# Moving three score tiles and one transpose block in the TensorE order of a fused attention and mixture-of-experts kernel

## The chip, the cores and the metric

The kernel runs on one core of one Trainium2 chip. The metric is device time in microseconds (us) of one execution. The core has five engines that run their own instruction streams in order and wait for each other through semaphores: TensorE (PE in the rows; its weight loads are PEld), VectorE (DVE), ScalarE (ACT), GpSimd (POOL) and SyncE (SP), which issues loads.

## The reference, cut to what matters

Attention with normalised queries and keys feeds a mixture-of-experts layer; q, k and v are 8 x 12 x 448 x 64 in float32 (batch, heads, tokens, head size).

```
q_n, k_n = rmsnorm(q, g_q), rmsnorm(k, g_k)
scores   = (q_n @ k_n.T) / sqrt(64)
x        = softmax(scores) @ v              # 3584 tokens x 768
y_dense  = relu(x @ w1_dense) @ w2_dense    # 768 -> 512 -> 768
expert   = argmax(x @ w_gate)               # 8 experts
y_moe    = gate * (relu(x @ w1[expert]) @ w2[expert])
out      = y_dense + y_moe                  # 3584 x 768, float32
```

## The kernel before, in words

**Units of work.** The 12 heads of a batch are three groups of four heads, so there are 24 groups, g = 0 to 23. A group has seven score tiles, s0 to s6. `scores` (L336 to L350) makes one: TensorE writes a tile of 128 x 2 x 448 into one of two PSUM buffers called `sc`, and ScalarE takes its exponential into `xflat`, which frees the buffer. A tile takes two matmuls, each over 64 of the 128 rows of the array; s3 takes four, each over a quarter of the array. `attend` (L366) multiplies the exponentials with the values into the PSUM tile `AV`, `division` divides, `xtrans` (L407) turns the result, x, with eight transposes into bank 1 of the PSUM tile `W`, and `xturned` copies it to `xT`. `logits` (L425) are eight small matmuls for the gate.

**Preparing a group.** GpSimd adds the squares up (`ss`, L290, from the square `m` that ScalarE makes at L288), ScalarE makes the scale r from it with a logarithm and an exponential (`ln`, L294, and `r`, L296), GpSimd multiplies with r (`xn`, L302, four instructions a group), and TensorE turns the product with 28 transposes (L313) into both banks of `W`. They are followed on TensorE by value products and the next score tiles. On GpSimd's queue stand, between the `xn` of one group and the `ss` of the next, a scatter of finished records (L488) and two casts of v (L267).

**Dense chunks.** When a batch's x is there, its 448 tokens go through `w1_dense` in four chunks of 128, 128, 128 and 64 tokens (`dense`, L616): six matmuls of 512 columns a chunk, accumulated in one bank of `W`; `relu` (L624) on ScalarE takes the sum out and frees the bank. The first and third chunk use bank 0, the second and fourth bank 1. The chunks of a batch are spread over the score tiles of the following batches' groups. Below, **place A** is the second chunk, **place B** the third. Both occur in the six batches from the first to the sixth while scores still run.

**What sets the order.** All instructions of the attention part are issued in the order of a list of times (`AT`, L16 on). A group is 7 units of that time long; an entry is an offset, one for each of the three kinds of group (g mod 3). `s0` to `s6` give the score tiles, `de` the chunks: for each its bank, its parts as (time, first matmul, last matmul + 1), the time of its relu and of its scatter. An instruction's place on every engine follows from that order; TensorE and ScalarE run theirs in it strictly. After 161 units the order is a written list, `tail`. The part behind it works through expert tiles on TensorE.

Of the kernel before, what the change touches and what calls it, by code (L numbers as in the profile page):

```python
# [17 lines left out]
AT = {'p00': [-0.862, 1.524, -1.092],  # L18
# [28 lines left out]
 'own': {1: -12.564, 2: 120.5, 13: 150.009, 14: 144.215, 15: 158.423, 16: None, 17: None, 18: None},  # L47
 'bl': 11.7,
 'last': 25,
# [39 lines left out]
def kernel(  # L89
# [94 lines left out]
    tail = const.tile([P, NT, 2], I32)  # L184
# [91 lines left out]
    def stats(g, name, s0, s1):  # L276
        if g >= NG:
            return []
        if g not in sts:
            sts[g] = sb.tile([P, 2, J, 2, 3], F32, tag="st", name="st")  # L280
        return [lambda s=s: nc.vector.bn_stats(  # L281
            sts[g][:, "qk".index(name), s].rearrange("p h c -> p (h c)"),
            xin[name, g].rearrange("p h (s d) -> p s d h", d=D)[:, s]) for s in range(s0, s1)]
# [14 lines left out]
    def normalise(g, name, hh, eng=None, r=None):  # L298
        r = rs[g] if r is None else r
        if (name, g) not in xn:  # L300
            xn[name, g] = sb.tile([P, J, 2, D], BF16, tag="xn" + name, name="xn", bufs=1)
        (eng or nc.gpsimd).tensor_tensor(  # L302
            xn[name, g][:, :, hh], xin[name, g][:, hh].rearrange("p (s d) -> p s d", d=D),
            r[:, "qk".index(name), :, hh].unsqueeze(2).to_broadcast([P, J, D]), ALU.mult)
# [78 lines left out]
    def division(g, r):  # L383
        b, gb = divmod(g, NB)
        if gb == 0 and r == 0:
            xas[b] = rb[b % 3][:, :, :XH].bitcast(BF16)
            xTs[b] = xT2[b % 2]
        claim("av", ("av", g, r))
        inv = sb.tile([P, 2, 4, 1], F32, tag="inv", name="inv")
        x = xas[b][:, :, gb * 256:gb * 256 + 256].rearrange("p m (a h i) -> p h m a i", a=2, h=4)  # L390

        def head(hh):
            on("AV", nc.vector.tensor_tensor(  # L393
                x[:, 2 * hh + r], av[:, hh, :, :D].rearrange("p m (a i) -> p m a i", a=2),
                inv[:, hh].unsqueeze(3).to_broadcast([P, 4, 2, 32]), ALU.mult), hh)
            if hh == 1:
                free(("av", g, r))

        return [lambda: on("AV", nc.vector.reciprocal(inv, av[:, :, :, D:]), 0, 1), lambda: head(0),
                lambda: head(1)]  # L400
# [74 lines left out]
    def places(b):  # L475
        rk = W[:, 1, RK:].rearrange("p (m e) -> p m e", e=E)
        at = ats[b % 2]

        def summed():
            with nc.allow_low_precision(reason="whole numbers"):  # L480
                nc.vector.tensor_reduce(slot[b % 2], at, AX.X, ALU.add)

        return [lambda: (on("W", nc.vector.tensor_tensor(at[:, :, :E], rk, oh[:, b, :4], ALU.mult),
                            1), free(("ra", b))),
                summed]
# [179 lines left out]
    def put(t, key, n, make):  # L665

        got = []

        def run(i):
            if not got:  # L670
                got.extend(make())
                assert len(got) == n, (key, n, len(got))
            got[i]()

        t0, dt = t if isinstance(t, tuple) else (t, 0.001)
        for i in range(n):
            todo.append((t0 + i * dt, len(todo), key, lambda i=i: run(i)))

    def put1(t, key, f, *a):
        put(t, key, 1, lambda: [lambda: f(*a)])  # L680
# [7 lines left out]
    def shift(t, z):  # L688
        return (t[0] + z, t[1]) if isinstance(t, tuple) else t + z

    def at(name, z, g):
        t = AT[name]
        return shift(t[g % NB] if isinstance(t, list) else t, z)

    def attention():
        for g in range(NG):
            z = J * g
            if g:
                for s in range(J):
                    put1(at("s%d" % s, z - J, g), ("s", g, s), scores, g, s)  # L700
            for r in range(2):
                for i, (m0, m1) in enumerate(((0, 2), (2, 4))):
                    put1(at("p%d%d" % (r, i), z, g), ("p", g, r), attend, g, r, m0, m1)
                put(at("d%d" % r, z, g), ("d", g, r), 3, lambda g=g, r=r: division(g, r))
            put1(at("xt", z, g), ("xt", g), xtrans, g)
            put1(at("xe", z, g), ("xe", g), xturned, g)
            put1(at("lo", z, g), ("lo", g), logits, g)
            if g > 1:
                put1(at("tr", z - 14, g), ("tr", g), transposes, g)
                put1(at("tq", z - 14, g), ("tq", g), turned_q, g)  # L710
                put1(at("tk", z - 14, g), ("tk", g), turned_k, g)
                put1(at("va", z - 7, g), ("va", g), values, g)
            if g > 2:
                put(at("st", z - 21, g), ("st", g), 14,
                    lambda g=g: stats(g, "k", 0, 7) + stats(g, "q", 0, 7))
                put1(at("me", z - 21, g), ("me", g), means, g)
                put1(at("no", z - 21, g), ("no", g), norms, g)
                put(at("nm", z - 21, g), ("nm", g), 4, lambda g=g: [
                    lambda name=name, hh=hh: normalise(g, name, hh)
                    for name in AT["kq"] for hh in range(2)])  # L720
                put1(at("lv", z - 14, g), ("lv", g), load_v, g)
            if g > 4:
                put1(at("lq", z - 35, g), ("lq", g), load_q, g)
                if g % 2 == 0:
                    put1(at("lk", z - 35, g), ("lk", g), load_k, g)
        for b in range(B):
            z = J * NB * (b + 1)
            put(at("ch", z, 0), ("ch", b), 8, lambda b=b: choose(b))
            put1(at("ra", z, 0), ("ra", b), ranks, b)
            put(at("pl", z, 0), ("pl", b), 2, lambda b=b: places(b))  # L730
            put(at("ga", z, 0), ("ga", b), 4, lambda b=b: gates(b))
            for m, bank, ks, re, se in AT["de"]:
                for t, k0, k1 in ks:
                    put1(z + t, ("de", b, m), dense, b, m, bank, k0, k1)
                put1(z + re, ("re", b, m), relu, b, m, bank)
                put1(AT["sx"].get((b, m), z + se), ("se", b, m), scatter, b, m)
        for n, job in enumerate(wjobs):
            if n >= 1:
                t = AT["we"][0] + (n - 3) * AT["we"][1]
                if n in AT["own"]:  # L740
                    t = AT["own"][n]
                if t is not None:
                    put1(t, ("we", n), nc.gpsimd.dma_start, *job)
        put(AT["el"], ("el",), 21, early_list)
        put1(AT["bl"], ("bl",), blank)
        todo.sort()
        for t, _, key, f in todo:
            if t < J * (NG - 1):
                f()
            else:  # L750
                left.setdefault(key, []).append(f)
# [286 lines left out]
    with tc.manual_schedule(engines=ENGINES):  # L1038
        prologue()
        attention()  # L1040
        tail_and_slots()
# [42 lines left out]
```

## Time and profile before

| what | us |
|---|---|
| median of 3 runs | 353.22 |
| lowest and highest run | 351.29, 355.0 |
| the profiled execution, its own time | 350.3 |
| its span on the core | 348.6 |
| TensorE busy in the span | 312.8 |
| ScalarE busy in the span | 212.8 |
| attention with dense chunks under way, about | 56 to 200 |
| expert tiles, about | 212 to 345 |

An engine's busy time is the time in which at least one of its instructions runs. Matmuls overlap each other, so a busy TensorE is not one at its peak. Times in the rows are counted from the start of the span.

### The profile page before, as it was taken

Reading aid. Unit: us, or ns where it says so; the run is one execution under the profiler, and the core shown is the slowest. Engines: PE = TensorE matmul, PEld = TensorE weight load, DVE = VectorE, ACT = ScalarE, POOL = GpSimd, SP = SyncE. Lnnn points to the kernel's source line nnn. Section 1 sums busy time; section 2 is a strip of 40 time slices with the busy share of each in tenths; the row PEclk is TensorE's granted clock in tenths of the full one; section 3 lists DMA queues with packets and bytes.
Section 4 is the critical chain, followed back from the end, with each engine's and each line's share of the span. In section 5 each row is a group of like instructions: output and inputs, shape, how many; then the busy total and the mean of one; then the engine's idle time right before and its main releaser. Section 6 shows DMA issues by size and latency. Waiting matters only on the chain. (4 is left out here: it accounts for less than half of the span.)

```text
span 348.6 us, 11328 instructions
## 1 busy us (share of the span) xinstructions
PE 312.8 (90%) x4164; PEld 192.7 (55%) x4164; DVE 231.4 (66%) x835; ACT 212.8 (61%) x348; POOL 202.2 (58%) x290
## 2 busy tenths in 40 slices
PE   0389989989989899999899899999999999999990
PEld 0255656656656565666666556555555555555550
DVE  5988998878988879888898744258222226364641
ACT  2389998898898898998988834322332332323220
POOL 4666887788886987988987522462323221322222
PEclk9999999999999999999999999999999999999997
DMA  7999999999997999989999799999999948495422
GB/s 263 265 249 240 311 291 210 289 259 323 233 305 240 256 300 253 285 227 253 262 276 192 166 186 182 259 282 248 176 248 240 212 121 205 123 182 140 123 93 80
DMA packets 83406, 78.85 MB, mean 226 GB/s; under 512 B 46894, under 2 KB 76088, under 8 KB 83344
## 3 DMA queue, kind: packets, MB, share of 16 engines
q1 hardware_dynamic: 69360, 42.58, 50.8%
q0 software_dynamic: 13984, 35.47, 40.5%
q8 instruction: 36, 0.59, 0.7%
q14 instruction: 26, 0.21, 0.2%
HBM read 61.40 MB, written 23.02 MB: 242 GB/s over the span
## 5 line engine op out<-in xcount | busy, mean ns | idle before, releaser
L350 ACT ACTIVATE xflat<-sc 128x896 bf16<-128x896 f32 x168 | 143.8, 918 | 6.0 <-PE sc L348 5.4
L302 POOL TENSOR_TENSOR xn<-we,r 128x448 bf16<-128x448 f32 x90 | 82.0, 945 | 14.5 <-issue 6.8
L348 PE MATMUL sc<-qT,kT 64*128 64x448 bf16 (+1 forms) x384 | 65.9, 372 | 12.0 <-ACT xflat L350 8.8
L366 PE MATMUL AV<-va,xflat 128*128 128x65 bf16 (+1 forms) x1536 | 75.7, 195 | 0.5 <-ACT xflat L350 0.4
L281 DVE BATCH_NORM_STATS2 st<-we 128x6 f32<-128x128 f32 x336 | 70.3, 280 | 2.9 <-DMA we<-in_k_dram 2.8
L366 PEld LDWEIGHTS <-xflat 128*128 128x128 bf16 (+1 forms) x1536 | 59.9, 98 | 22.2 <-issue 12.1
L929 POOL DMA_INDIRECT out_dram<-xflat,tail x22 | 22.7, 1032 | 64.5 <-DVE xflat L928 52.4
L928 DVE COPY xflat<-yp 128x768 f32<-128x768 f32 x22 | 21.0, 956 | 46.3 <-PE yp L898 46.3
L878 ACT COPY heT<-AV 128x512 bf16<-128x512 bf16 x26 | 15.2, 585 | 55.3 <-PE AV L874 55.3
L488 POOL DMA_INDIRECT records<-rall,slot x32 | 33.1, 1036 | 23.7 <-ACT rall L624 18.0
L616 PE MATMUL W<-wd,xT 128*128 128x512 bf16 (+1 forms) x240 | 42.8, 339 | 0.7 <-DVE kT L334 0.7
L898 PE MATMUL yp<-we,heT 128*128 (+1 forms) x232 | 42.5, 326 | 0.0
L348 PEld LDWEIGHTS <-kT 64*128 64x128 bf16 (+1 forms) x384 | 24.1, 97 | 28.3 <-issue 22.0
L393 DVE TENSOR_TENSOR rall<-AV,inv 128x256 bf16<-128x256 f32 x96 | 36.3, 420 | 1.7
L859 PE MATMUL W<-we,xflat 128*128 (+1 forms) x132 | 32.6, 379 | 0.3 <-issue 0.2
L624 ACT ACTIVATE rall<-W 128x512 bf16<-128x512 f32 (+1 forms) x40 | 20.3, 509 | 19.9 <-PE W L616 18.4
L887 PE MATMUL yp<-wd,xflat 128*128 128x384 bf16 x176 | 32.2, 327 | 0.0
L864 ACT ACTIVATE hs<-W,tail 128x512 bf16<-128x512 f32 x26 | 17.9, 687 | 23.1 <-PE W L859 19.5
L898 PEld LDWEIGHTS <-heT 128*128 128x128 bf16 (+1 forms) x304 | 22.5, 97 | 15.0 <-issue 1.0
L267 POOL CAST va<-we 128x448 bf16<-128x448 f32 x48 | 26.9, 593 | 0.0
L616 PEld LDWEIGHTS <-xT 128*128 128x128 bf16 (+1 forms) x240 | 16.8, 102 | 15.3 <-issue 4.4
L887 PEld LDWEIGHTS <-xflat 128*128 128x128 bf16 x176 | 16.9, 98 | 14.1 <-issue 1.3
(151 smaller groups left out, 348.6 us busy)
## 6 DMA issues: line engine op xcount, KB each, us to landing
we<-in_moe_w_dram POOLq DMA_DIRECT2D x16, 768.0 KB, 10.0
we<-in_q_dram SPq DMA_DIRECT2D x24, 448.0 KB, 9.6
we<-in_k_dram SPq DMA_DIRECT2D x11, 896.0 KB, 8.2
we<-in_v_dram SPq DMA_DIRECT2D x48, 128.0 KB, 9.6
we<-in_v_dram SPq DMA_DIRECT2D x48, 96.0 KB, 7.2
wd<-in_moe_w_dense_dram POOLq DMA_DIRECT2D x2, 768.0 KB
we<-in_k_dram SPq DMA_DIRECT2D x2, 448.0 KB, 3.5
records<-rall,slot POOLq DMA_INDIRECT x32, 6.6
```

The costliest lines, as they stand in the source:

```text
L267: nc.gpsimd.tensor_copy(vas[g % 3][:, :, :, a * 32:a * 32 + 32].rearrange("p s h i -> p h s i"), xin["v", g].rearrange("p h (s i a) -> p h ...
L281: return [lambda s=s: nc.vector.bn_stats(sts[g][:, "qk".index(name), s].rearrange("p h c -> p (h c)"), xin[name, g].rearrange("p h (s d) - ...
L302: (eng or nc.gpsimd).tensor_tensor(xn[name, g][:, :, hh], xin[name, g][:, hh].rearrange("p (s d) -> p s d", d=D), r[:, "qk".index(name), : ...
L348: nc.tensor.matmul(ps[out, hh, :S], kT[row, w:w + out.stop - out.start], qT[row, r], start=True, stop=True, skip_group_check=True)
L350: nc.scalar.activation(x, ps[:, :, :S], AF.Exp, scale=scale)
L366: on("AV", nc.tensor.matmul(av[:, hh, m], exs[g, s][rows_, hh, QC[m]:QC[m] + P], va[rows_, s, hh, :De], start=(first and s == full[0] and ...
L393: on("AV", nc.vector.tensor_tensor(x[:, 2 * hh + r], av[:, hh, :, :D].rearrange("p m (a i) -> p m a i", a=2), inv[:, hh].unsqueeze(3).to_b ...
L488: i = nc.gpsimd.indirect_dma_start(out=rec, out_offset=bass.IndirectOffsetOnAxis(ap=slot[b % 2][:, m:m + 1], axis=0), in_=rb[b % 3][:, m], ...
L616: on("W", nc.tensor.matmul(o, xTs[b][:, kk, q0:QC[m] + P], wd1[:, kk, c], start=(kk == 0), stop=(kk == KD - 1), skip_group_check=(m == 3)) ...
L859: got = [nc.tensor.matmul(he[c], xRs[t][:, kk, c], matrix(t, 0, h, kk * F, (kk + 1) * F), start=(kk == 0), stop=(kk == KD - 1)) for h, c i ...
L887: nc.tensor.matmul(yps[t][:, dd, :HD], xRs[t][:, KD + i], wd2[:, i, dd * HD:(dd + 1) * HD], start=(i == 0), stop=False, skip_group_check=True)
L898: return [nc.tensor.matmul(yp[c, dd, :HD], heTs[t][:, i, c], matrix(t, 1, h, cols.start, cols.stop), start=False, stop=(i == FT - 1), skip ...
```

## The change

Three entries of the table change, and one is new.

- At place A the tile s3 of the group that follows (offset 0.9, now 0.65) comes between the second and the third matmul of the second dense chunk. It stood behind that chunk's relu.
- At place B the third dense chunk is cut in two parts, matmuls 0 and 1 and matmuls 2 to 5, and the tile s0 of the group that follows (offset 0.455, now -0.4) comes between them. It stood behind the chunk and behind the eight logits matmuls. Of group 4, which has no chunk there, s0 moves ahead of eight logits matmuls.
- `xtrans` of group 22, the eight transposes of the last but one turn of x, stands at 160.9 in the list of times, ahead of logits and the first value products of group 23. In `tail` it stood behind them and behind two loads of expert numbers.

```diff
- 'de': ... (2, 0, [(20.56, 0, 6)], 20.943, 27.29), (3, 0, [(26.48, 0, 6)], 28.824, 32.5)],
+ 'de': ... (2, 0, [(20.56, 0, 2), (20.62, 2, 6)], 20.943, 27.29), (3, 0, [(26.48, 0, 6)], 28.824, 32.5)],
+ 'xs': {22: 160.9},
- 's0': [-0.586, 0.455, 2.566],
+ 's0': [-0.586, -0.4, 2.566],
- 's3': [0.9, 0.991, 3.16],
+ 's3': [0.65, 0.991, 3.16],
- 'tail': [..., ('nu', 0), ('nu', 1), ('xt', 22), ('de', 6, 2), ...
+ 'tail': [..., ('nu', 0), ('nu', 1), ('de', 6, 2), ...
-            put1(at("xt", z, g), ("xt", g), xtrans, g)
+            put1(AT["xs"].get(g, at("xt", z, g)), ("xt", g), xtrans, g)
```

The changed kernel has one line more above these functions, so its lines have numbers higher by one. The instructions of VectorE, GpSimd and SyncE stand as before; those of TensorE and ScalarE move.

TensorE at place A of one batch, before: the last two of the chunk's six matmuls (L616) and the four matmuls of s3 (L348) behind them.

```order
L616 LDWEIGHTS xT_82
L616 MATMUL W<-wd_88,xT_82 128x512
L616 LDWEIGHTS xT_82
L616 MATMUL W<-wd_88,xT_82 128x512
L348 LDWEIGHTS kT_92
L348 MATMUL sc<-qT,kT_92 64x448
L348 LDWEIGHTS kT_92
L348 MATMUL sc<-qT,kT_92 64x448
L348 LDWEIGHTS kT_92
L348 MATMUL sc<-qT,kT_92 64x448
L348 LDWEIGHTS kT_92
L348 MATMUL sc<-qT,kT_92 64x448
```

The same place now: the first two of the six, then s3, then the other four (one of them shown).

```order
L617 LDWEIGHTS xT_82
L617 MATMUL W<-wd_88,xT_82 128x512
L349 LDWEIGHTS kT_92
L349 MATMUL sc<-qT,kT_92 64x448
L349 LDWEIGHTS kT_92
L349 MATMUL sc<-qT,kT_92 64x448
L349 LDWEIGHTS kT_92
L349 MATMUL sc<-qT,kT_92 64x448
L349 LDWEIGHTS kT_92
L349 MATMUL sc<-qT,kT_92 64x448
L617 LDWEIGHTS xT_82
L617 MATMUL W<-wd_88,xT_82 128x512
```

So the four remaining matmuls of the chunk, and with them its relu, come behind s3.

ScalarE over places A and B of one batch, before: `xflat<-sc` are exponentials of score tiles, the two `rall<-W` rows the relus of place A and place B.

```order
L350 ACTIVATE xflat<-sc 128x896 x2
L624 ACTIVATE rall<-W 128x512
L350 ACTIVATE xflat<-sc 128x896 x2
L288 ACTIVATE m_1471<-st 128x28
L350 ACTIVATE xflat<-sc 128x896
L294 ACTIVATE ln<-ss,eps_t 128x28
L296 ACTIVATE r<-ln 128x28
L350 ACTIVATE xflat<-sc 128x896 x2
L624 ACTIVATE rall<-W 128x512
L350 ACTIVATE xflat<-sc 128x896 x3
```

The same stretch now.

```order
L351 ACTIVATE xflat<-sc 128x896 x3
L625 ACTIVATE rall<-W 128x512
L351 ACTIVATE xflat<-sc 128x896
L289 ACTIVATE m_1471<-st 128x28
L351 ACTIVATE xflat<-sc 128x896
L295 ACTIVATE ln<-ss,eps_t 128x28
L297 ACTIVATE r<-ln 128x28
L351 ACTIVATE xflat<-sc 128x896 x3
L625 ACTIVATE rall<-W 128x512
L351 ACTIVATE xflat<-sc 128x896 x2
```

Each of the two relus now has one more exponential ahead of it and one fewer behind it.

## Rows read from the trace of the kernel before

**Rows 1.** Page, part 1: busy us, share of the span, instructions.

```profile
PE 312.8 (90%) x4164; PEld 192.7 (55%) x4164; DVE 231.4 (66%) x835; ACT 212.8 (61%) x348; POOL 202.2 (58%) x290
```

**Rows 2.** Windows: attention, expert tiles; busy us by engine (instructions), clock, DMA.

```profile
56.00:200.00 144.00, 135.75 (x2403) 88.04 (x2401) 121.90 (x486) 127.04 (x208) 120.00 (x161) 1.00 0.99 256
212.00:320.00 108.00, 106.99 (x772) 61.03 (x770) 44.81 (x108) 33.77 (x55) 33.00 (x35) 1.00 0.93 204
```

**Rows 3.** ScalarE's waits, 56 to 200: us in total, times, longest.

```profile
ACT rall L624 <- PE W L616: 11.7, 18, 1.0
ACT xflat L350 <- PE sc L348: 2.5, 9, 0.9
```

**Rows 4.** TensorE's waits, 56 to 200.

```profile
PE sc L348 <- ACT xflat L350: 5.8, 11, 1.0
```

**Rows 5.** Lines by form: a dense matmul of 512 columns; busy, mean ns | idle before.

```profile
L616 PE MATMUL W<-wd,xT 128*128 128x512 bf16 x144 | 36.2, 381 | 0.0
```

**Rows 6.** Timeline of TensorE over places A and B of one batch: start, us, what.

```profile
83.07 1.47 PE L616 MATMUL W<-wd,xT 128*128 128x512 bf16 x6
84.47 0.68 PE L348 MATMUL sc<-qT,kT 64*64 64x448 bf16 x6
84.98 0.80 PE L313 MATMUL W<-ident,xn 64*128 64x64 bf16 x28
...
86.34 0.35 PE L348 MATMUL sc<-qT,kT 64*128 64x448 bf16 x1
...
89.15 1.47 PE L616 MATMUL W<-wd,xT 128*128 128x512 bf16 x6
...
90.74 0.68 PE L348 MATMUL sc<-qT,kT 64*128 64x448 bf16 x6
...
92.11 0.36 PE L348 MATMUL sc<-qT,kT 64*128 64x448 bf16 x2
92.30 0.58 PE L313 MATMUL W<-ident,xn 64*128 64x64 bf16 x28
```

**Rows 7.** Timeline of ScalarE, same batch; in brackets idle time before and its releaser.

```profile
84.58 0.60 ACT L624 ACTIVATE rall<-W 128x512 bf16<-128x512 f32 x1 [0.77 <-PE W L616]
85.07 1.72 ACT L350 ACTIVATE xflat<-sc 128x896 bf16<-128x896 f32 x2
86.66 0.25 ACT L288 ACTIVATE m<-st 128x28 f32<-128x28 f32 x1
86.79 0.93 ACT L350 ACTIVATE xflat<-sc 128x896 bf16<-128x896 f32 x1
...
87.96 0.23 ACT L296 ACTIVATE r<-ln 128x28 f32<-128x28 f32 x1
...
90.66 0.60 ACT L624 ACTIVATE rall<-W 128x512 bf16<-128x512 f32 x1 [0.86 <-PE W L616]
...
94.55 0.32 ACT L294 ACTIVATE ln<-ss,eps_t 128x28 f32<-128x28 f32 x1
```

**Rows 8.** Timeline of GpSimd, same batch.

```profile
88.31 3.64 POOL L302 TENSOR_TENSOR xn<-we,r 128x448 bf16<-128x448 f32 x4 [1.07 <-ACT r L296]
92.11 1.06 POOL L488 DMA_INDIRECT records<-rall,slot  x1 [0.16 <-issue]
...
94.26 0.26 POOL L290 TENSOR_TENSOR ss<-st,m 128x28 f32<-128x28 f32 x1
```

**Rows 9.** Timeline of TensorE: a score matmul and the fourth chunk behind it.

```profile
94.74 0.35 PE L348 MATMUL sc<-qT,kT 64*128 64x448 bf16 x1
95.02 0.85 PE L616 MATMUL W<-wd,xT 128*64 128x256 bf16 x12
```

**Rows 10.** Timeline of ScalarE, the batch before that one.

```profile
70.64 0.32 ACT L294 ACTIVATE ln<-ss,eps_t 128x28 f32<-128x28 f32 x1 [0.74 <-POOL ss L290]
```

**Rows 11.** Timeline of GpSimd, the fifth of the six batches.

```profile
161.70 3.63 POOL L302 TENSOR_TENSOR xn<-we,r 128x448 bf16<-128x448 f32 x4 [1.34 <-DMA we<-in_v_dram]
```

**Rows 12.** Timeline of TensorE: transposes of group 22 behind loads of expert numbers.

```profile
205.31 0.62 PE L407 MATMUL W<-ident,rall 128*128 128x128 bf16 x8 [0.82 <-issue]
```

4 rows, old and new, of the table AT are left out of this document.

## The prediction

> **What bounds the kernel now.** I read the page's busy shares first. TensorE is busy for 90% of the span [rows 1]; that is an average over two stages, so the windows come next. From 212 us on TensorE is busy 106.99 of 108 us [rows 2]: whatever reaches it late there ends late, and a microsecond lost or won in attention comes out at the end as one. In attention, 56 to 200 us, TensorE (135.75 of 144), ScalarE (127.04), VectorE (121.90) and GpSimd (120.00) are all nearly full, at full granted clock. So busy shares decide nothing there and the waits must be read. ScalarE waits 11.7 us for dense chunks, 18 times, and 2.5 us for score tiles [rows 3]; TensorE waits 5.8 us for ScalarE to free a score buffer, 11 times [rows 4]. Each engine waits for the other, at different points of a batch. That is what the change aims at: while six dense matmuls run, ScalarE has emptied both score buffers and stands idle, 0.77 us at place A and 0.86 us at place B of one batch [rows 7]. The question is what comes after these two places, and I followed one batch engine by engine.
>
> **Prices on TensorE.** A dense matmul takes 0.38 us [rows 5], and six of them 1.47 [rows 6], so they start (1.47 - 0.38) / 5 = 0.218 us apart. The last one at A starts at 84.54 - 0.38 = 84.16, and s3 starts at 84.47: 0.31 after it, so going from full-array matmuls to score matmuls costs 0.09 over the pace. From s3 to the next tile it is 85.15 - 0.36 - 84.47 = 0.32; from a score matmul to a dense one 95.02 - 94.74 = 0.28 [rows 9]. A tile in the middle of a chunk thus costs one such passage more, 0.09 us, and the rest of the chunk ends 0.3 us plus that later. No row shows a tile in the middle of an accumulation; the bounds are 0 (the passage hides under the weight loads) and 0.16 a passage (the next matmul starts only when the last has ended, 0.38 - 0.22). I take 0.09, the price of the same passage at the end of a chunk.
>
> The Trainium skill has a rule that speaks against the change: TensorEngine Tiling (Array Packing), section Key Properties, says that switching the tiling mode drains TensorE. Here 0.31 us stands where a full drain would need the 0.38 us of the matmul ahead, so the trace agrees that a switch costs something and not that it empties the array. By the rule at its strictest each passage would cost 0.16 us instead of 0.09.
>
> **Place A, step by step** [rows 6 to 8]. Before: the chunk runs from 83.07 to 84.54, its relu from 84.58 to 85.18. In the shadow of the relu TensorE does s3 and the next tile (84.47 to 84.98) and starts the 28 transposes of the next group. These write both banks, so from the second on they wait for the relu; they take 0.80 us here and 0.58 us at 92.30, where nothing holds them: a stall of 0.22. Then come value products and the tile s1, whose second matmul (86.34) lets ScalarE go on at 86.79; r follows at 87.96.
> Now: two dense matmuls (83.07, 83.29), s3 at 83.60, the other four at 83.92, 84.14, 84.35 and 84.57, end 84.95 instead of 84.54, the next tile at 84.88 instead of 84.79. ScalarE has s3 at about 84.01, so most of its idle 0.77 is filled. But the relu starts at 84.99 and ends at 85.59, **0.41 later**; the stall of the transposes grows from 0.22 to 0.54, and everything behind them on TensorE is 0.41 late. ScalarE, with one exponential fewer behind the relu, reaches the square m at about 86.27 instead of 86.66, 0.39 early, and then waits: s1 ends at 86.34 + 0.41 + 0.35 = 87.10, its exponential starts at 87.14 instead of 86.79. So r is 0.35 late. What was hidden under the relu (s3 on TensorE) has been moved ahead of it, and what waits for the relu pays.
>
> **Where the 0.35 goes.** GpSimd stood idle 1.07 us for r and starts `xn` 0.12 after r has ended (88.31). Behind it the queue is close to gapless: four `xn` (3.64), the scatter at 92.11, two casts, `ss` at 94.26 to 94.52, and ScalarE's `ln` starts at 94.55. In the batch before, `ln` even waited 0.74 us for `ss` [rows 10]. So 0.35 late at r is about 0.3 late at the next `ln`, and behind that ScalarE runs through to the next place A. Four of the six batches look like this one (`xn` after an idle of 1.07). In the fifth the idle is 1.34 and ends with something else, a load of v [rows 11]: it takes up 0.27 of the delay, I count 0. In the sixth the delay stays on TensorE, which is the bound from there on: 0.4.
>
> **Place B** [rows 6, 7]. s0 starts at 89.37 + 0.31 = 89.68 instead of 90.74; the chunk ends 0.4 later, and logits and s3 keep their place within 0.1. No transposes wait for this relu: the next 28 come at 92.30, when even a relu that ends 0.4 later than 91.26 is through. ScalarE fills most of its 0.86, and the third exponential could start about 0.3 earlier. But the next `ln` waits for `ss` of GpSimd, which was set by r back at A; what B gives ScalarE is given back there. I count 0, with bounds of +0.1 (the passage) and -0.3 a batch (if `ln` could follow).
>
> **The rest.** s0 of group 4 passes eight small logits once: 0, within 0.2. The eight transposes of group 22 take 0.62 us and stand behind an idle of 0.82 us in which TensorE's sequencer loads two expert numbers [rows 12]. They move ahead of value products on the same engine; the loads stay behind the same products, so the idle stays. VectorE's copy of the turned x comes earlier, but nothing on TensorE waits for it. I count 0, between -0.8 (the idle goes) and +0.5 (the transposes are no longer ahead of a chunk but in a place where they wait).
>
> **Sum.** 4 x 0.3 + 0 + 0.4 = +1.6 us. The profiled execution took 350.3 us and would take 351.9. It lies 2.9 us under the median of the three runs, 353.22; on that the forecast is **354.8 us**. A difference under 1%, 3.5 us, can't be told from none in this kernel, so this is forecast as no change that shows, on the slower side. Chance 0.5, with its own range of 353.5 to 356.2.
>
> **Rivals.**
> - *ScalarE is the bound and its idle time comes back.* For: 11.7 us of waits for dense chunks, and TensorE's 5.8 us for ScalarE, which say that later in the batch ScalarE is last. Then the 0.39 that m is early at A and the 0.3 at B count, 6 x 0.69 = 4.1, 349.1 us. Against: s1 behind the transposes on TensorE. It decides for this rival if the second of the 28 transposes at A starts no later than now after the chunk began, 85.22 - 83.07 = 2.15 us (85.22 being the relu's end and the 0.04 us that it also took from the chunk's end to the relu). Half of it, with A lost and B kept, is 351.3. Chance 0.17, a third of it over 1%.
> - *The delay is taken up on the way.* TensorE's 5.8 us of waits for ScalarE are slack for TensorE, and GpSimd may catch up in more batches than the fifth; then only the last 0.4 or so stays, 353.2 to 354.0. Chance 0.2.
> - *The passages cost a full matmul and nothing takes them up.* A then is 0.41 + 2 x 0.07 = 0.55 late, B 0.16 late on TensorE: 6 x 0.71 = 4.3, 357.5 us, slower by 1.2%. For: the weights of a score tile and of a dense matmul replace each other in mid-accumulation, which no row shows. Against: 0.31 and 0.28 [rows 6, 9]. It decides from 0.16 us a passage on. This is also what the Trainium skill's rule on the drain (named above) gives. Chance 0.13.
>
> **Range and chances.** The likeliest case alone gives 353.5 to 356.2; to hold 8 in 10 the range reaches down to half of the first rival and to a run or two of scatter (the three runs lie within 3.7 us), and up to the last: 350.6 to 357.4. Faster by over 1%: 0.09, from the first rival and scatter; slower by over 1%: 0.13, from the last rival and scatter on the forecast; within 1%: 0.78.
>
> **What would show it.** In the changed profile the relu at A starts about 1.92 us after its chunk's first matmul instead of 1.51, with ScalarE's idle before it near 0.2; the 28 transposes behind it take near 1.1 us instead of 0.80; GpSimd's idle for r grows from 1.07 towards 1.8 (its `ss` comes 0.39 earlier and r 0.35 later); ScalarE waits near 0.6 us for s1 behind the square. At B the relu's idle shrinks from 0.86 and `ln` waits longer for `ss`. A place A comes about 0.3 us later each batch than before. The prediction is wrong if GpSimd's `xn` starts earlier after the chunk than the 5.24 us of now (88.31 - 83.07), or if place A of successive batches comes closer together; then ScalarE was the bound after all.

## The result and the profile after

The kernel before has a median of 353.17 us in 22 runs, the changed one 357.97 us in 22 runs. In half of the changed kernel's runs the time is 7 us to 21 us longer than in its shortest, in some of the kernel before 6 us to 48 us, and the comparison leaves these runs out. Of the others the ratio is **1.0066, 95% interval 1.004 to 1.0091**: +2.3 us (1.4 to 3.2) on some 352. The lowest runs, 352.77 and 350.77 us, say +2.0. The forecast was 354.8 us, +1.6, on the slower side and too small to show, in a range of 350.6 to 357.4. The median of the runs that are compared, 354.34 us, lies in it; that of all 22, 357.97, lies just above it.

The execution that was profiled has a span of 372.0 us, and only its attention part is read against the kernel before. The window of the expert tiles shows why [rows 2]; the columns are as there.

```profile
212.00:320.00 108.00, 90.76 (x601) 51.47 (x608) 34.70 (x97) 28.76 (x48) 28.18 (x31) 0.92 1.11 171
```

TensorE is busy for 90.76 of 108 us there, not 106.99, at a granted clock of 0.92. In attention the waits have changed places. ScalarE's waits, 56 to 202 us, after [rows 3]:

```profile
ACT xflat L351 <- PE sc L349: 10.9, 27, 0.8
ACT ln L295 <- POOL ss L291: 1.8, 2, 1.1
ACT rall L625 <- PE W L617: 0.3, 1, 0.3
```

The 11.7 us of waits for dense chunks are gone, as intended, and 10.9 us of waits for score tiles have come, where 2.5 were. TensorE's waits in the same stretch [rows 4]:

```profile
PE sc L349 <- ACT xflat L351: 4.2, 9, 0.9
PE W L314 <- issue: 1.3, 4, 0.4
PE W L314 <- ACT rall L625: 1.1, 3, 0.4
```

L314 are the 28 transposes; the last two rows hold their waits at the six places A, up to 0.4 us each, and one of 0.2 us behind a place B. At place A the profile names the relu (L625) three times and three times nothing ("issue"). The timeline of TensorE shows the two places of one batch [rows 6]. The second matmul of each cut chunk has no record in this trace.

```profile
83.67 0.39 PE L617 MATMUL W<-wd,xT 128*128 128x512 bf16 x1
84.20 0.38 PE L349 MATMUL sc<-qT,kT 64*64 64x448 bf16 x4
84.52 1.04 PE L617 MATMUL W<-wd,xT 128*128 128x512 bf16 x4
...
85.69 0.19 PE L314 MATMUL W<-ident,xn 64*128 64x64 bf16 x1
86.24 0.56 PE L314 MATMUL W<-ident,xn 64*128 64x64 bf16 x27 [0.36 <-issue]
...
87.36 0.35 PE L349 MATMUL sc<-qT,kT 64*128 64x448 bf16 x1
...
90.39 0.38 PE L617 MATMUL W<-wd,xT 128*128 128x512 bf16 x1 [0.16 <-issue]
90.71 0.36 PE L349 MATMUL sc<-qT,kT 64*128 64x448 bf16 x2
91.00 1.04 PE L617 MATMUL W<-wd,xT 128*128 128x512 bf16 x4
```

ScalarE in the same batch [rows 7]:

```profile
84.64 0.92 ACT L351 ACTIVATE xflat<-sc 128x896 bf16<-128x896 f32 x1 [0.23 <-PE sc L349]
85.59 0.60 ACT L625 ACTIVATE rall<-W 128x512 bf16<-128x512 f32 x1
...
86.88 0.24 ACT L289 ACTIVATE m<-st 128x28 f32<-128x28 f32 x1
87.74 0.92 ACT L351 ACTIVATE xflat<-sc 128x896 bf16<-128x896 f32 x1 [0.61 <-PE sc L349]
...
88.89 0.23 ACT L297 ACTIVATE r<-ln 128x28 f32<-128x28 f32 x1
...
92.08 0.60 ACT L625 ACTIVATE rall<-W 128x512 bf16<-128x512 f32 x1
```

And GpSimd [rows 8]:

```profile
87.21 0.24 POOL L291 TENSOR_TENSOR ss<-st,m 128x28 f32<-128x28 f32 x1 [0.39 <-ACT m L289]
89.25 3.64 POOL L303 TENSOR_TENSOR xn<-we,r 128x448 bf16<-128x448 f32 x4 [1.80 <-ACT r L297]
```

Counted from the chunk's first matmul (83.07 us before, 83.67 now), the relu starts after 1.92 us instead of 1.51, the square m after 3.21 instead of 3.59, r after 5.22 instead of 4.89, and `xn` after 5.58 instead of 5.24. ScalarE waits 0.61 us for the score tile that stands behind the transposes on TensorE. (The prediction calls that tile s1; it is s4 of its group.)

From one place A to the next (start of the relu) the traces give, in us:

| kernel | 1 to 2 | 2 to 3 | 3 to 4 | 4 to 5 | 5 to 6 | 1 to 6 |
|---|---|---|---|---|---|---|
| before | 24.72 | 24.12 | 24.81 | 24.15 | 24.25 | 122.05 |
| before, once more (`e8_before_again`) | 24.74 | 24.14 | 24.84 | 24.90 | 24.24 | 122.87 |
| the change | 25.05 | 24.47 | 25.15 | 25.09 | 24.57 | 124.33 |
| the change, once more (`e1_whole`) | 25.08 | 24.46 | 25.18 | 25.07 | 24.59 | 124.38 |

The second trace of the kernel before is needed here: the 24.15 of the fourth period stands in the first trace alone (why is read under `e8_before_again`). Against the second trace the five periods lose 0.31, 0.33, 0.31, 0.19 and 0.33 us. From the batch's first relu to the first at A 3.72 us pass instead of 3.30, and from the sixth at A to the first expert matmul 28.63 instead of 28.73 (the first trace; the second takes 30.19, at a lower granted clock). That is +1.5 + 0.4 - 0.1 = **+1.8 us** up to the expert tiles.

This sum is put together from two traces, since each of them alone holds something that is not the change's. From the first relu to the first expert matmul the kernel before takes 154.08 and 156.34 us, `e4_turn_22`, which moves nothing in these batches, 154.91, the change 156.68 and 156.78. So the change alone is +2.6 against one trace, +0.3 against the other and +1.8 against `e4_turn_22`: the periods and offsets batch by batch say more than these totals.

### The profile page after: what moved, and what is told of

Its sections match the earlier page's. It is cut to its first block, busy times and chain, and to the rows that moved or that the text cites. A ratio compares the mean times of both kernels' runs of the same rounds, so it can differ in the third digit from the quotient of the medians.

```text
span 372.0 us, 11293 instructions
## 1 busy us (share of the span) xinstructions
PE 313.2 (84%) x4129; PEld 193.0 (52%) x4164; DVE 230.5 (62%) x835; ACT 216.5 (58%) x348; POOL 202.2 (54%) x290
## 4 chain that ended last, share of the span: by engine, by line
PE 39%; DMA 10%; ACT 5%; SPq 5%; DVE 3%; issue 3%; DVEq 1%; POOL 0%; POOLq 0%; ACTq 0%
DMA rall<-records 9%; PE yp L888 7%; PE yp L899 6%; PE W L617 6%; PE W L860 6%; PE AV L367 5%; ACT xflat L351 4%; PE sc L349 4%; SPq L799 3%; PE W L408 2%; ACT rall L625 1%; DMA xflat<-records 1%; PE mid L860 1%; DVE rall L833 1%; SPq L798 1%
## 5 line engine op out<-in xcount | busy, mean ns | idle before, releaser
L351 ACT ACTIVATE xflat<-sc 128x896 bf16<-128x896 f32 x168 | 145.9, 917 | 14.9 <-PE sc L349 13.6
L349 PE MATMUL sc<-qT,kT 64*128 64x448 bf16 (+1 forms) x384 | 67.3, 371 | 12.5 <-ACT xflat L351 7.5
L617 PE MATMUL W<-wd,xT 128*128 128x512 bf16 (+1 forms) x219 | 41.6, 335 | 3.0 <-issue 1.9
L860 PE MATMUL W<-we,xflat 128*128 (+1 forms) x121 | 30.5, 379 | 0.7 <-issue 0.2
L625 ACT ACTIVATE rall<-W 128x512 bf16<-128x512 f32 (+1 forms) x40 | 20.4, 509 | 9.5 <-PE W L617 7.2
L617 PEld LDWEIGHTS <-xT 128*128 128x128 bf16 (+1 forms) x240 | 15.9, 102 | 15.8 <-issue 7.7
```

The lines of the kernel that those rows point to most:

```text
L349: nc.tensor.matmul(ps[out, hh, :S], kT[row, w:w + out.stop - out.start], qT[row, r], start=True, stop=True, skip_group_check=True)
L351: nc.scalar.activation(x, ps[:, :, :S], AF.Exp, scale=scale)
L617: on("W", nc.tensor.matmul(o, xTs[b][:, kk, q0:QC[m] + P], wd1[:, kk, c], start=(kk == 0), stop=(kk == KD - 1), skip_group_check=(m == 3)) ...
L860: got = [nc.tensor.matmul(he[c], xRs[t][:, kk, c], matrix(t, 0, h, kk * F, (kk + 1) * F), start=(kk == 0), stop=(kk == KD - 1)) for h, c i ...
```

## The experiments

The theory: place A alone loses, since its relu comes 0.41 us later and the 28 transposes, s4 and r queue behind it; place B and the turn of x move nothing. The rivals: the switches between dense and score matmuls cost TensorE time at both places; or place B takes back what A loses.

**e1_whole**: the change itself, on the chip of the next three.

> The whole change once more, beside its parts on one chip. Theory (the relu of place A stands in the path: s3 has left its shadow, the transposes wait for it, and value products, the next tile, r and GpSimd's queue follow): +1.5 to +3 us, and in the profile the relu of A about 0.41 us later than before against the m = 0 relu of the same batch, the transposes behind it taking 1.1 us. Rival 1 (ScalarE's idle time comes back): not slower. Rival 3 (passages between tiling modes): the rest of a chunk behind a tile ends over 0.5 us late at A and at B.

Measured: 1.0111 (1.0017 to 1.0205), which is +3.9 us with a wide interval; lowest run 354.28 us against 350.52. Its offsets at A are those shown above: the relu starts 1.93 us after the chunk, the transposes take 1.12 us, m comes at 3.22, r at 5.23.

**e2_place_A**: place A alone.

```diff
- 's3': [0.9, 0.991, 3.16],
+ 's3': [0.65, 0.991, 3.16],
```

> Only s3 in the middle of the second chunk; place B, s0 of group 4 and the transposes of group 22 as before. Theory: all of the loss is here, +1.5 to +3 us, as much as the whole change within 0.7 us. Rival 1: a gain of up to 2.3 us (0.39 x 6). Rival 3: half of the loss, since half of the twelve places have the tile in the chunk.

Measured: 1.004 (0.9958 to 1.0122), too wide to tell by time. The trace tells: periods of 25.09, 24.48, 25.17, 25.03 and 24.61 us, 124.37 in all, the whole change's 124.38. Each period is within 0.04 us of that of `e1_whole`, so place B and the turn of group 22 add nothing to place A. TensorE at place A of the second batch, with all its records:

```profile
83.57 0.60 PE L616 MATMUL W<-wd,xT 128*128 128x512 bf16 x2
84.10 0.38 PE L348 MATMUL sc<-qT,kT 64*64 64x448 bf16 x4
84.42 1.04 PE L616 MATMUL W<-wd,xT 128*128 128x512 bf16 x4
...
85.59 0.19 PE L313 MATMUL W<-ident,xn 64*128 64x64 bf16 x1
86.14 0.56 PE L313 MATMUL W<-ident,xn 64*128 64x64 bf16 x27 [0.36 <-issue]
```

The second dense matmul starts at 83.57 + 0.60 - 0.38 = 83.79, s3 0.31 after it, the third dense matmul 0.32 after s3. So a switch inside a chunk costs what it costs at the end of one. The chunk ends at 85.46 instead of 83.57 + 1.47 = 85.04.

**e3_place_B**: place B alone.

```diff
- (2, 0, [(20.56, 0, 6)], 20.943, 27.29)
+ (2, 0, [(20.56, 0, 2), (20.62, 2, 6)], 20.943, 27.29)
- 's0': [-0.586, 0.455, 2.566],
+ 's0': [-0.586, -0.4, 2.566],
```

> Only s0 in the middle of the third chunk (and s0 of group 4 ahead of eight logits); place A and the transposes of group 22 as before. Theory: 0, within 0.7 us, because no one waits for that relu and what ScalarE gains it gives back waiting for ss. Rival 1: a gain of up to 1.8 us (0.3 x 6). Rival 3: half of the loss, about +1 to +1.5 us.

Measured: 1.0021 (0.9947 to 1.0096). The first three periods are 24.71, 24.11 and 24.81 us, those of the kernel before to 0.03. The fifth (25.21) has a wait of VectorE for a load of q in it, 1.97 us, and isn't read; the fourth (25.33) has none and is read below. ScalarE, at place B of the second batch and at the `ln` of the third:

```profile
90.33 0.92 ACT L350 ACTIVATE xflat<-sc 128x896 bf16<-128x896 f32 x1 [0.30 <-PE sc L348]
91.30 0.60 ACT L624 ACTIVATE rall<-W 128x512 bf16<-128x512 f32 x1
...
119.80 0.32 ACT L294 ACTIVATE ln<-ss,eps_t 128x28 f32<-128x28 f32 x1 [1.14 <-POOL ss L290]
```

The relu's idle 0.86 is nearly gone (0.30 ahead of the exponential before it), and `ln` waits 1.14 us for `ss` where the kernel before waits 0.84 at that `ln`. What ScalarE gained it waits for there. In the first two batches that wait is as before (0.78 for 0.74, and none): ScalarE comes to m 0.27 us early, but to the exponential behind it only 0.03 and 0.05 early, after idle times of 0.14 and 0.12 for which the profile names nothing. In all three batches `ln` starts 0.03 to 0.04 us after `ss` has ended, and as far from the chunk at A as in the kernel before (12.28, 11.47 and 12.38 us, to 0.01), so an earlier ScalarE could not have moved it.

The fourth period is 0.43 longer than in the second trace of the kernel before, in which a score tile behind place A stops as it does here (see `e8_before_again`). TensorE, behind place B of that batch:

```profile
142.88 0.22 PE L313 MATMUL W<-ident,xn 64*128 64x64 bf16 x2 [0.22 <-issue]
...
143.64 0.97 PE L366 MATMUL AV<-va,xflat 128*128 128x65 bf16 x13 [0.36 <-DVE rall L393]
```

It stops ahead of the last two of the 28 transposes, with nothing named, and waits for VectorE's division behind them. Neither trace of the kernel before has these two waits; the change and `e1_whole` have both in the same batch (0.17 and 0.21, then 0.36), though their period there is only 0.06 and 0.04 longer than with place A alone. So the zero for place B holds in three batches and not in this one, and what stops the two transposes is not shown.

**e4_turn_22**: the turn of x for group 22 alone.

```diff
+ 'xs': {22: 160.9},
- 'tail': [..., ('nu', 0), ('nu', 1), ('xt', 22), ('de', 6, 2), ...
+ 'tail': [..., ('nu', 0), ('nu', 1), ('de', 6, 2), ...
-            put1(at("xt", z, g), ("xt", g), xtrans, g)
+            put1(AT["xs"].get(g, at("xt", z, g)), ("xt", g), xtrans, g)
```

> Only the eight transposes of group 22 ahead of logits and value products; places A and B as before. Theory: 0, within 0.5 us, the 0.8 us of idle time for the two loads of expert numbers stay, now right ahead of the dense chunk. Rival: the idle time is gone, -0.8 us.

Measured: 1.0015 (0.9961 to 1.0068); its periods are those of the second trace of the kernel before to 0.06, 122.85 us in all, the 24.96 of the fourth among them. TensorE before the expert tiles [rows 12]:

```profile
203.85 0.62 PE L408 MATMUL W<-ident,rall 128*128 128x128 bf16 x8
204.31 0.34 PE L426 MATMUL AV<-wgb,xT 128*128 128x8 bf16 x8
204.51 0.77 PE L367 MATMUL AV<-va,xflat 128*128 128x65 bf16 x16
206.13 3.54 PE L617 MATMUL W<-wd,xT 128*128 128x512 bf16 x24 [0.86 <-issue]
```

The turn stands ahead of the value products without a wait, and the idle time of 0.82 us has stayed where the number loads are: 0.86, now ahead of the chunk.

**e5_A_late_transposes**: place A, and the 28 transposes moved one stage of value products back, behind s4, so that the relu is through when they start.

```diff
- 'tr': [2.755, 1.399, 2.327],
- 'tq': [3.163, 3.396, 3.158],
+ 'tr': [2.755, 3.92, 2.327],
+ 'tq': [3.163, 3.93, 3.158],
- 's3': [0.9, 0.991, 3.16],
+ 's3': [0.65, 0.991, 3.16],
```

> Place A as in the change, and the 28 transposes that waited for its relu moved behind the next value products and the tile after them (with the copy of q behind them on VectorE). Theory: the wait for the relu is covered, so the 0.36 us a batch of e2 go and ScalarE's early exponentials count: place A to place A of the next batch no longer than before, the whole between -1.0 and +0.5 us. Rival 3 (the passages themselves are the loss): still as slow as e2, about +1.5 us or more, because the same passages are there. Rival 1 expects nothing different from e2.

Measured: 1.0024 (0.9982 to 1.0066); 122.73 us from the first to the sixth place A. With place A alone it was 124.37, before 122.05 and 122.87. TensorE, the second batch:

```profile
84.71 0.69 PE L366 MATMUL AV<-va,xflat 128*128 128x65 bf16 x13
...
85.41 0.68 PE L313 MATMUL W<-ident,xn 64*128 64x64 bf16 x28
...
87.53 0.61 PE L407 MATMUL W<-ident,rall 128*128 128x128 bf16 x8 [0.54 <-DVE kT L334]
```

The relu is as late as in place A alone (1.93 us after the chunk's start), but the transposes take 0.68 instead of 1.12 and r starts 4.50 us after the chunk, not 5.23. Value products now stand where the transposes waited. So the loss of place A is the transposes' wait and what queues behind it. By time the result is +0.8 us (-0.6 to +2.3), above the expected -1.0 to +0.5 but not clear of it. A new wait has come: TensorE stands idle 0.54 us for VectorE's copy of kT, which frees the bank for the turn of x.

**e6_late_transposes**: the late transposes without place A (the first four lines of the diff above).

> Only the 28 transposes moved behind the value products and the next tile, the tiles at A and B as before. Theory: no gain, since they waited just 0.2 us for the relu; instead the copies of q and k on VectorE come about 0.7 us later and x's transposes, which need the bank, wait for them: 0 to +2 us, so that a gain of e5 against e2 is not the move's own. Rival (the move is a gain by itself): -0.2 x 6 = -1.2 us.

Measured: 1.0064 (1.002 to 1.0107), 124.19 us. By themselves the late transposes lose nearly as much (1.3 us against the 122.87) as place A does by itself (1.5). Only the two together are level, so the two losses don't add up.

**e7_AB_late_transposes**: places A and B with the late transposes (the edits of e3 and e5).

> Places A and B as in the change, the transposes moved as in e5, those of group 22 as before. Theory: the best order of these, since at B ScalarE's early exponential also counts when the transposes no longer hold r back: -1.5 to +0.3 us. Rival 3: slower than e5 by the passages of place B, about +1 us.

Measured: 1.0039 (0.9999 to 1.0078), 123.45 us. That is +1.4 us (0 to 2.7), where -1.5 to +0.3 was expected: a miss. Place B adds nothing that helps; the last two periods (24.90, 24.95) are 0.2 and 0.7 longer than those of e5. In the fifth batch stands the stop that e3 has in the fourth, ahead of the last two of the 28 transposes behind place B (0.16 us, nothing named), and the wait of 0.36 for VectorE's division behind it. Why it comes in this batch is not shown.

**e8_before_again**: the kernel before as a run of its own.

> The kernel before once more, as a kernel of its own: ratio 1 within its interval, and a second trace in which the distances from place A to place A show how far they repeat from one execution to the next. All theories: the same distances within 0.1 us, but for places where a load lands late.

Measured: 1.0019 (0.9982 to 1.0057), which is what an equal kernel gives here. The one period in which its trace differs from the first (24.90 against 24.15, the fourth) has these rows on TensorE:

```profile
134.75 0.36 PE L348 MATMUL sc<-qT,kT 64*128 64x448 bf16 x1
134.78 0.26 PE L366 MATMUL AV<-va,xflat 64*128 64x65 bf16 x3
135.27 0.35 PE L348 MATMUL sc<-qT,kT 64*128 64x448 bf16 x1 [0.16 <-issue]
```

The second matmul of s4 starts 0.52 us after the first, with nothing named for it; in the first trace's rows of that batch it is 0.13. r is 0.32 later than there, about as late as with the change, and the batch is 0.75 longer. The same stop stands in the traces of e3 and e4. With r that late the eight transposes of x wait for VectorE's copy of kT in this batch, and in the fourth batch of the change they do so too, though no score matmul stops there; in the first trace they don't. This trace, then the change:

```profile
136.83 0.61 PE L407 MATMUL W<-ident,rall 128*128 128x128 bf16 x8 [0.31 <-DVE kT L334]
```

```profile
138.51 0.61 PE L408 MATMUL W<-ident,rall 128*128 128x128 bf16 x8 [0.29 <-DVE kT L335]
```

So in the fourth batch a late r goes with a further wait of 0.3 us. Against the first trace the change loses 0.94 there; the 0.19 against the second is small only because that trace was late for a reason of its own.

The 30.19 us behind the sixth place A have another cause. TensorE from 200 to 204 us, in the first trace and in this one, columns as in [rows 2]:

```profile
200.00:204.00 4.00, 4.00 (x73) 2.75 (x70) 2.43 (x12) 2.27 (x5) 0.00 (x0) 1.00 0.93 136
```

```profile
200.00:204.00 4.00, 4.00 (x44) 2.46 (x44) 1.92 (x12) 1.69 (x3) 0.09 (x1) 0.61 0.88 133
```

The granted clock is 0.61 on average and 0.50, the lower level of 1.2 GHz, from 200 to 203 us; TensorE gets through 44 matmuls instead of 73. In the microseconds 197 to 199 it had been busy for 0.71 and 0.51, in the first trace, whose clock stays at 1.00, for 0.71 and 0.57.

**e9_A_turn_late**: e5, with the eight transposes of x behind one more score tile, to fill the 0.54.

```diff
- 'xt': [11.96, 12.342, 14.734],
- 'xe': [12.836, 12.616, 15.279],
+ 'xt': [11.96, 12.95, 14.734],
+ 'xe': [12.836, 13.0, 15.279],
```

> Place A with late transposes, and the eight transposes of x of that group (which stand behind the 28) moved behind one more score tile. With place A and late transposes alone TensorE stood idle 0.54 us ahead of them in each of six batches, 3.3 us in all, for VectorE's copy of kT. If that wait is TensorE's loss, the score tile fills 0.3 of it, six times: 1.8 us faster than place A with late transposes, a period of 24.2 to 24.5 in place of 24.4 to 24.8, and about 0.4 to 0.5% under the kernel before. If ScalarE or GpSimd set the period, the wait goes and comes back as a wait for ScalarE: no change, a ratio of 1.002.

Measured: 1.0022 (0.9976 to 1.0067), no faster than the kernel before by time. In the trace 121.79 us from the first to the sixth place A, 0.9 less than e5: half of the 1.8. It comes from two of the five periods (24.33 for 24.76, 24.29 for 24.72); the others move by 0.09 at most, though the wait shrinks in every batch. The wait for kT is smaller, not gone (1.6 us in six times instead of 3.3):

```profile
86.36 0.63 PE L348 MATMUL sc<-qT,kT 64*128 64x448 bf16 x3
87.25 0.61 PE L407 MATMUL W<-ident,rall 128*128 128x128 bf16 x8 [0.26 <-DVE kT L334]
```

**e10_A_middle_transposes**: e9, with the 28 transposes ahead of s4 instead of behind it.

```diff
- 'tr': [2.755, 3.92, 2.327],
+ 'tr': [2.755, 3.9, 2.327],
```

> As the run before, and the 28 transposes ahead of s4 instead of behind it: they start where the relu at place A has just ended, so they stall by less than 0.1 us. If the stall for the late relu alone makes place A lose, r comes 0.2 to 0.3 later than with transposes behind s4 (4.75 us after the chunk in place of 4.50, against 4.89 before) and nothing is lost to the kernel before: within 0.3%, place A to place A 122.5 to 123. If one more score tile ahead of the chunk's end costs by itself, it is like place A alone: 124.4, slower by 0.5%.

Measured: 1.0001 (0.9963 to 1.0039), 122.25 us, a little under the expected 122.5 to 123. The transposes take 0.69 us, and r comes 4.69 us after the chunk, between the 4.50 of e9 and the 5.23 of place A alone. The tile in the middle of the chunk is still there, and the loss is not: again the wait for the relu, not the passages. The later turn of x from e9 is in this order too, so the total is not the work of the transposes' place alone.

**e11_AB_turn_late**: e9 and place B.

> The first of these runs with place B of the change too. If what B gives ScalarE (0.86 us of idle time) is given back at ln, which waits for GpSimd, the period does not move: within 0.3% of the first of these runs. If GpSimd, which now gets r 0.39 us earlier, no longer holds ln up, B brings 0.3 us a batch: 1.8 us, 0.5% faster than that run.

Measured: 0.9985 (0.9948 to 1.0022), lowest run 348.37 us against 349.23 for the kernel before; 121.41 us from the first to the sixth place A, 0.4 less than e9. Of the five periods two are shorter than in e9 (by 0.29 and 0.14), the others equal. In these two, and in the fifth batch, `ln` comes 0.26 us earlier after the chunk; in the first and the third batch it waits for GpSimd again, in the third:

```profile
119.72 0.32 ACT L294 ACTIVATE ln<-ss,eps_t 128x28 f32<-128x28 f32 x1 [0.34 <-POOL ss L290]
```

So with r early B is worth 0.29 us at best and 0.08 us a batch on average, not 0.3. Up to the expert tiles this version is 153.25 us from its first relu, the change 156.68: 3.4 us less. The kernel before takes 154.08 there (156.34 in the trace with the lower clock) and e4 154.91; that is 0.8 to 1.7 us more than this version, and by run time they can't be told apart. No version here beats the kernel before by more than the measurement is uncertain.

## Why the prediction was right, and where it was not

**Right: the mechanism and its sizes at place A.** The relu starts 1.92 us after the chunk's first matmul (forecast 1.92), the transposes take 1.11 (1.12), m is 0.38 early (0.39), r 0.33 late (0.35), GpSimd's idle time grows to 1.80 (1.8), ScalarE waits 0.61 for s4 (0.6). The idle time of 0.2 comes as 0.23, ahead of s3's exponential and not of the relu. The price of 0.09 us a passage holds: the chunk in e2 ends 85.46 - 85.04 = 0.42 late, forecast 0.41. By the rule of the Trainium skill, TensorEngine Tiling (Array Packing), Key Properties, at its strictest (a mode switch drains TensorE) it would be an estimated 0.55. The trace does not agree with that reading: 0.31 and 0.32 us from start to start leave no room for waiting out the 0.38 us that the profile gives the matmuls ahead.

**Right: the zeros for place B and the turn of x, with one batch that doesn't fit.** e3 leaves the first three periods where they were, e4 all five, and with place A in the kernel B moves none of the five (`e1_whole` against e2). In both the reason is the one given: `ln` starts when `ss` has ended (its wait grows from 0.84 to 1.14 in the third batch), and the idle time for the number loads stays (0.86). In the whole change the longest wait of `ln` for `ss` is 1.1 us, in the third batch too. The 0.43 us of the fourth batch of e3 were not foreseen; the prediction counted on transposes behind place B that go through.

**Mis-sized: the fifth batch.** The step said that the idle time of 1.34 us on GpSimd "ends with something else, a load of v: it takes up 0.27 of the delay, I count 0". It lost 0.33. ScalarE's r and GpSimd's `xn` in that batch; before:

```profile
161.05 0.23 ACT L296 ACTIVATE r<-ln 128x28 f32<-128x28 f32 x1
```

With the change (`e1_whole`), r and `xn` behind it:

```profile
165.37 0.23 ACT L297 ACTIVATE r<-ln 128x28 f32<-128x28 f32 x1
```

```profile
166.03 1.84 POOL L303 TENSOR_TENSOR xn<-we,r 128x448 bf16<-128x448 f32 x2 [1.66 <-issue]
```

Before, `xn` starts 161.70 - 161.28 = 0.42 us after r has ended [rows 11]; with the change 166.03 - 165.60 = 0.43, and 0.42 or 0.43 it is in all thirteen traces, in which r comes in this batch between 4.50 and 5.23 us after the chunk. If a load had set that start, it would not keep to r so closely. The profile names the load, but `xn` followed r here as in the other batches, only 0.3 us more slowly (0.13 there). What these 0.3 us are the rows don't show (after the change they are "issue"). The trace of the kernel before already held a warning. In the first batch the profile names the same load, and there too `xn` starts 0.13 us after r has ended (63.47):

```profile
63.60 3.64 POOL L302 TENSOR_TENSOR xn<-we,r 128x448 bf16<-128x448 f32 x4 [1.07 <-DMA we<-in_v_dram]
```

**The sum.** Forecast 4 x 0.3 + 0 + 0.4 = 1.6. Measured up to the expert tiles: 0.31, 0.33, 0.31, 0.19, 0.33, and 0.42 - 0.1 = 0.32 for the sixth: 1.8. That the two are so close is in part luck: the fifth batch lost 0.33 where 0 was counted, and the fourth only 0.19 because the second trace of the kernel before has lost time there already. Against the first trace the fourth loses 0.94, with a wait for VectorE's copy of kT (0.29) in it that the prediction doesn't have. The ratio of the runs says 2.3 with an interval of 1.4 to 3.2, which holds both sums.

**The rivals.** ScalarE as the bound needed the second transpose within 2.15 us of the chunk's start; it comes at 86.24 - 83.67 = 2.57, and `xn` comes 0.34 later, not earlier. A delay that is taken up on the way is refuted by the periods, passages at the price of a full matmul by e2 (0.42 where they would give 0.55).

## What to carry to other kernels

When work is moved ahead of a step to fill an idle engine, ask what waits for that step: here ScalarE's idle time was filled, and the transposes that reuse the relu's bank paid for it. Moved out of its way they no longer waited for it, though a new wait, for VectorE's copy, took most of the gain. A wait that ends last by the profile isn't always the one that binds: see whether the start keeps its distance to the other input when that input moves. And where a trace has a number on which a term rests, a second trace of the same kernel tells whether it is the rule: 24.15 and 24.90 us stood in the same place.

## What the runs showed that was not expected

The part with the expert tiles, in which these edits move nothing, varied by more than all the edits moved. In the trace of the changed kernel TensorE waits there for reads of records, in that of `e1_whole` for a write of the output, in the kernel before for neither. The longest waits from 213 us on, after:

```profile
PE W L860 <- DMA rall<-records: 16.2, 2, 9.0
```

and in `e1_whole`:

```profile
PE W L860 <- DMA out_dram<-xflat,tail: 3.5, 1, 3.5
```

In the 108 us from 212 us on the granted clock averaged 0.92 in the trace of the changed kernel and 1.00, 2.4 GHz, in that of the kernel before [rows 2]. In the changed kernel TensorE stood idle for 7.15 and 9.04 us, up to 261.70 and 276.33 us; in both waits the clock fell to 0.50, 1.2 GHz, and it was back at 1.00 from about 265 and 282 us on. So TensorE worked some 8.6 us at half the clock, which cost an estimated 4.3 us. With 17.1 us of waits for records that makes 21.4, against 20.6 us by which the part from the first expert matmul on is longer than in the kernel before. Whether the order of the attention part changes how often such waits come, no run shows.
